# A retention layer followed by a mixture of attention experts: a new order of work in the head, at one step in the middle, and in the tail

## The chip, the cores and the metric

The kernel runs on one core of one Trainium2 chip. Its engines work side by side, each through its own instructions in program order: PE (matmuls), DVE, ACT and POOL (elementwise work), SP (which here only issues DMA transfers). What is measured is the time of one execution on the device in microseconds (us); lower is better.

## The reference

Eight batches of 576 tokens, eight heads of 64. First a retention layer, that is linear attention with a decay and no softmax; its output, 512 wide, is the input of a layer of four attention experts, of which each token takes two, weighted by a gate.

```python
scale = 1.0 / np.sqrt(64)
scores = scale * (q @ k.transpose(0, 1, 3, 2))
Dmat = np.where(rel >= 0, gamma[:, None, None] ** rel, 0.0)    # rel = i - j
x = (scores * Dmat) @ v          # then heads side by side: [8, 576, 512]
logits = x @ w_gate              # 4 experts, the two largest, softmax over them
for e in range(4):
    q, k, v = x @ wq[e], x @ wk[e], x @ wv[e]
    s = np.where(causal, -1e9, (q @ k.transpose(0, 2, 1)) / 8)
    a = np.exp(s - s.max(-1)); a /= a.sum(-1)
    out += chosen_weight[e] * (a @ v @ wo[e])
```

## The kernel before, in words

**Order.** Every engine runs its instructions in the order in which the program writes them; waits between engines are semaphores set from the tiles that are read and written. PSUM is a pool of eight banks that all stages take in turn (`bank`), so a matmul can also wait for a bank whose last reader isn't done. What stands where is decided by hand: a head written out line by line, a loop over n = 4 to 36 with a table of what each step does (`TILES` for scores, `STEPS` for the rest), and a `tail` written out again. Generators (`yield`) cut a stage in pieces, and `run`, `next` and `beside` say where a piece goes.

**Retention.** The batches go in four pairs, the tokens of a pair in nine steps of 128 columns, 36 steps in all. For a step n, `load(n)` brings x (queries and keys) and vk (values and keys) by DMA into three buffers each. `qk` multiplies keys by queries, ACT copies the result p, POOL sets it to zero above the diagonal (`affine_select`, L130). `decay` scales vk by powers of gamma (L95: DVE up to step 5, POOL later), `state` multiplies it to a state st, which DVE adds to the running state s (L111, L113). `result` has PE multiply the old state by the queries (old) and p by the values (own), adds the two (ACT L158, DVE L173), multiplies by the table gi (L178: DVE for n up to 2, POOL later) and splits the result in xh (ACT L181) and its remainder xl (L183), since a matmul takes rounded inputs: every product with x or a weight is done as hi·hi + lo·hi + hi·lo. `build` fills gi step by step on ACT (L136).

**Experts.** Three groups R of 384 tokens to a pair. `fetch(w)` brings a weight into a part of the tile TA, `weights(w)` splits it (whk, wlk and so on: hi on ACT L209, lo on DVE L211). `proj` makes k and q (pj, L226), `vproj` v and the gate's logits (pv, L251), `gate` the weights of the experts on DVE in two parts, `gates(0)` and `gates(1)`. v goes out to memory (hv) and comes back turned (`back`: vq<-hv, four DMA issues on SP). A batch b has five tiles t of queries; `score` computes scores (ss, L354, for t = 4 L360), DVE masks them and finds the minimum (L369, nm), ACT takes exps with their sums (L377). A step later `factors` makes the factors on DVE, `scale` multiplies the rows by them on ACT (L395), `turn` transposes blocks of 32x32 on DVE into TA and TB (L403, L405). `values(b, s0, s1)` multiplies them by vq for all five tiles at once (ys, L418, 144 matmuls for the whole batch, of which each leaves two rows in the trace), ACT rounds the result to yh (L424), DVE takes the remainder yl (L425); of an even batch POOL copies the last half block to the front of the next (L428). `outproj(n)` multiplies 128 columns of y by the output weights (po, L440), ACT copies them to ot (L448) and SP sends them out.

**Cold PE.** `warm(6)` issues six dummy matmuls (pw, L69) on a bank of their own.

## Time and profile before

| | |
|---|---|
| median of three executions | 425.62 us (425.48 to 428.55) |
| profiled execution | 426.58 us |
| its span, first to last instruction | 424.7 us |
| mean granted clock of PE | 0.988 of full |
| PE busy | 393.2 us, 93% |
| ACT, DVE, POOL busy | 283.4, 265.3, 167.3 us |
| moved by DMA | 65.10 MB, 153 GB/s |

The profile is of one execution, which has its own time; it lies 0.96 us over the median. The span is counted from the first instruction to the last; 1.88 us lie around it. A share of busy time is a mean over stages: head, loop and tail have different limits.

### The profile page before, as it was taken

To read this page: it belongs to the slowest core of one execution; us is meant where nothing else is said; L and a number is where in the kernel's file an instruction comes from. 1 tells how busy PE (TensorE), PEld (TensorE's weight loads), DVE (VectorE), ACT (ScalarE), POOL (GpSimd) and SP (SyncE) were. 2 spreads that over 40 slices of the span, in tenths; PEclk is the share of its full clock that TensorE was granted. 3 is DMA by queue.
4 is the path that set the end of the run, shared out by engine and by line. 5 is a ranking of instruction groups with operands and counts; after the bars stand their busy time and mean duration, and the time that the engine had idled before them with its cause. 6 is when DMAs were issued, how large, how long until landed. Compare 5 with 4: busy or idle time off the path is not lost.

```text
span 424.7 us, 20358 instructions
## 1 busy us (share of the span) xinstructions
PE 393.2 (93%) x8742; PEld 333.8 (79%) x8742; DVE 265.3 (62%) x1103; ACT 283.4 (67%) x809; POOL 167.3 (39%) x182
## 2 busy tenths in 40 slices
PE   7597999996799999999998989999999999999894
PEld 3486898796688978897887978898788987887673
DVE  2745386765777726869296727677497726983931
ACT  4354469674597747878576747779587747797751
POOL 2217856443345534445354444444445432000000
PEclk9898999998999999999999999999999999999999
DMA  8568557464255536567264635566454221422331
GB/s 288 164 235 323 172 187 184 131 185 131 102 168 159 191 101 174 165 176 243 98 166 135 188 127 158 183 174 199 145 169 146 86 75 42 115 66 96 105 119 60
DMA packets 33689, 65.10 MB, mean 153 GB/s; under 512 B 3392, under 2 KB 19264, under 8 KB 33600
## 3 DMA queue, kind: packets, MB, share of 16 engines
q1 hardware_dynamic: 32304, 59.08, 44.4%
q10 hardware_dynamic: 1296, 4.72, 3.2%
q8 instruction: 69, 1.13, 1.2%
q14 instruction: 20, 0.16, 0.2%
HBM read 49.63 MB, written 14.16 MB: 150 GB/s over the span
## 4 chain that ended last, share of the span: by engine, by line
PE 83%; DVE 6%; issue 5%; DMA 3%; ACT 1%; SPq 1%; ACTq 1%; DVEq 0%
PE pj L226 25%; PE pv L251 13%; PE ys L418 12%; PE po L440 10%; PE ss L354 7%; PE qk L124 4%; PE own L168 4%; DMA vk<-vkf 3%; PE old L155 3%; PE st L106 3%; PE ss L360 2%; DVE yl L425 1%; DVE x L173 1%; DVE ta L403 1%; DVE p L369 1%
## 5 line engine op out<-in xcount | busy, mean ns | idle before, releaser
L377 ACT ACTIVATE p<-p,nm 128x64 f32<-128x64 f32 (+5 forms) x144 | 79.3, 552 | 18.0 <-DVE nm L369 13.4
L130 POOL TENSOR_SCALAR_AFFINE_SELECT p<-p 64x512 f32<-64x512 f32 x72 | 49.0, 680 | 95.4 <-ACT p L127 93.0
L395 ACT ACTIVATE p<-p,sm 128x64 f32<-128x64 f32 (+5 forms) x144 | 69.4, 567 | 9.5 <-DVE sm L389 5.6
L183 POOL TENSOR_TENSOR xl<-x,xh 128x512 fp32r<-128x512 f32 x33 | 42.4, 1284 | 60.5 <-ACT xh L181 60.5
L369 DVE CUSTOM_DVE_ANT_0 p<-ss,mask 128x128 f32<-128x128 f32 (+7 forms) x128 | 50.4, 452 | 4.4 <-PE ss L354 4.3
L173 DVE TENSOR_TENSOR x<-x,own 128x256 f32<-128x256 f32 (+1 forms) x72 | 25.5, 386 | 43.0 <-ACT x L158 35.7
L425 DVE TENSOR_TENSOR yl<-ys,yh 128x288 fp32r<-128x288 f32 (+2 forms) x36 | 12.8, 417 | 61.6 <-ACT yh L424 61.6
L178 POOL TENSOR_TENSOR x<-x,gi 128x512 f32<-128x512 f32 x33 | 42.5, 1289 | 18.2 <-DVE x L173 11.3
L403 DVE STREAM_TRANSPOSE ta<-p 128x256 f32<-128x256 f32 (+2 forms) x144 | 48.9, 367 | 0.2 <-ACT p L395 0.2
L418 PE MATMUL ys<-ta,vq 32*64 32x288 f32 (+6 forms) x1152 | 45.4, 365 | 3.8 <-issue 3.8
L418 PE MATMUL ys<-tb,vq 32*64 32x96 f32 (+4 forms) x1344 | 43.5, 248 | 5.0 <-issue 5.0
L418 PEld LDWEIGHTS ys<-tb,vq 32*64 32x64 f32 x1344 | 39.3, 134 | 7.2 <-issue 6.3
L418 PEld LDWEIGHTS ys<-ta,vq 32*64 32x64 f32 x1152 | 36.0, 133 | 8.4 <-issue 7.2
L354 PE MATMUL ss<-k,q 64*64 64x512 f32 (+7 forms) x512 | 38.5, 406 | 0.2 <-issue 0.2
L424 ACT ACTIVATE yh<-ys 128x288 fp32r<-128x288 f32 (+2 forms) x36 | 10.9, 389 | 38.1 <-PE ys L418 38.1
L448 ACT ACTIVATE ot<-po 128x512 f32<-128x512 f32 x35 | 19.9, 592 | 19.8 <-PE po L440 16.2
L95 POOL TENSOR_TENSOR vk<-vk,con 128x512 f32<-128x512 f32 x30 | 31.5, 1051 | 0.0
L127 ACT ACTIVATE p<-qk 128x256 f32<-128x256 f32 x72 | 23.7, 382 | 9.3 <-PE qk L124 8.3
L181 ACT ACTIVATE xh<-x 128x512 fp32r<-128x512 f32 x36 | 22.3, 618 | 10.5 <-POOL x L178 8.6
L106 PE MATMUL st<-vk 64*64 64x64 f32 x1024 | 24.1, 220 | 5.6 <-DVE vk L95 4.0
L113 DVE TENSOR_TENSOR s<-st,s 128x128 f32<-128x128 f32 x112 | 24.9, 281 | 6.2 <-PE st L106 6.2
L168 PE MATMUL own<-p,vk 64*64 64x64 f32 x1152 | 26.4, 222 | 2.0 <-issue 1.9
(86 smaller groups left out, 892.0 us busy)
## 6 DMA issues: line engine op xcount, KB each, us to landing
x<-xf SPq DMA_DIRECT2D x33, 512.0 KB, 4.5
vk<-vkf SPq DMA_DIRECT2D x33, 512.0 KB, 5.7
vq<-hv SPq DMA_DIRECT2D x48, 192.0 KB, 6.3
out<-ot SPq DMA_DIRECT2D x36, 256.0 KB, 2.3
hv<-vn SPq DMA_DIRECT2D x24, 192.0 KB, 2.6
ta<-wraw ACTq DMA_DIRECT2D x3, 512.0 KB, 5.6
x<-xf ACTq DMA_DIRECT2D x3, 512.0 KB, 4.3
vk<-vkf ACTq DMA_DIRECT2D x3, 512.0 KB, 6.2
```

What stands on the lines that cost most here:

```text
L130: gp.affine_select(w, w, pattern=[[0, 8], [1, 64]], base=0, channel_multiplier=-1, compare_op=OP.is_ge, fill=0.0)
L168: mm(own[r][HALF[u], g, i], vk[HALF[r], s, 0, 2 * g + u], p[HALF[r], g, s, u], start=True, stop=True)
L178: e.tensor_mul(x32, x32, gi[:, :, t0:t0 + 128])
L226: mm(ps, ww[:, kc, p * 128:(p + 1) * 128], xx[:, kc], start=(i == 0), stop=(i == 11))
L251: mm(ps, xx[:, kc, l0:l0 + 128], ww[:, kc], start=(i == 0), stop=(i == 11))
L354: mm(ps[u][HALF[p]], q(p, z, i), k[p][HALF[z], :ws[u]], start=True, stop=True)
L369: v.tensor_tensor_reduce(x, ps[u], mask[:, 512 - ws[u]:], -1.0, BIG, OP.add, OP.min, nm[:, u:u + 1])
L377: act(x, x, AF.Exp, bias=bias, scale=-1.0, accum_out=sm[:, 0, u:u + 1])
L395: act(x, x, AF.Copy, scale=sm[:, 1, u:u + 1])
L403: v.transpose(TA[:, :min(nb, 8), z, k], x[:, :min(nb, 8)])
L418: mm(py[g][HALF[z], sj - s0:], vq[QUAD[g], jj, D * z:D * z + D], tt[QUAD[g]], start=(m == 0), stop=(m == 2 * s1 - 1))
L440: mm(ps, yy[:, p], ww[:, p], start=(i == 0), stop=(i == 5))
```

## The change

**Head.** `state(1)` and `state(2)` are written ahead of the last parts of `result(0)` and `result(1)`, so their adds on DVE stand before the multiplication by gi and the remainder. On ACT, which also issues DMAs in the head, load(5) and the fetch of v's weights stand behind the first evacuation of k; before, that fetch stood ahead of it, and load(5) behind the four builds of gi. ACT from load(4) on, before (x_354 and k_420, q_422 are the step's x, k and q):

```order
L81 DMA x<-xf 128x1024
L85 DMA vk<-vkf 128x1024
L198 DMA ta<-wraw 128x1024
L235 ACTIVATE k_420<-pj 128x384
L238 ACTIVATE q_422<-pj 128x384
L127 ACTIVATE p<-qk 128x256 x2
L235 ACTIVATE k_421<-pj 128x384
L136 ACTIVATE gi<-gi,con 128x128 x4
L81 DMA x<-xf 128x1024
L85 DMA vk<-vkf 128x1024
```

And now:

```order
L83 DMA x<-xf 128x1024
L87 DMA vk<-vkf 128x1024
L241 ACTIVATE k_416<-pj 128x384
L83 DMA x<-xf 128x1024
L87 DMA vk<-vkf 128x1024
L200 DMA ta<-wraw 128x1024
L244 ACTIVATE q_418<-pj 128x384
L129 ACTIVATE p<-qk 128x256 x2
L241 ACTIVATE k_417<-pj 128x384
L138 ACTIVATE gi<-gi,con 128x128 x4
```

The second pair of x and vk issues has moved up five rows, the fetch (ta<-wraw) down three. On DVE the same head, from step 0's last sum on, before:

```order
L173 TENSOR_TENSOR x_175<-x_175,own 128x2x64
L178 TENSOR_TENSOR x_175<-x_175,gi 128x512
L113 TENSOR_TENSOR s<-st,s 128x128 x4
L95 TENSOR_TENSOR vk<-vk,con 128x2x256
L183 TENSOR_TENSOR xl<-x_175,xh 128x4x128
L173 TENSOR_TENSOR x_263<-x_263,own 128x2x128 x2
L178 TENSOR_TENSOR x_263<-x_263,gi 128x512
L183 TENSOR_TENSOR xl<-x_263,xh 128x4x128
L113 TENSOR_TENSOR s<-st,s 128x128 x4
```

And now:

```order
L175 TENSOR_TENSOR x_176<-x_176,own 128x2x64
L115 TENSOR_TENSOR s<-st,s 128x128 x4
L180 TENSOR_TENSOR x_176<-x_176,gi 128x512
L97 TENSOR_TENSOR vk<-vk,con 128x2x256
L185 TENSOR_TENSOR xl<-x_176,xh 128x4x128
L175 TENSOR_TENSOR x_264<-x_264,own 128x2x128 x2
L115 TENSOR_TENSOR s<-st,s 128x128 x4
L180 TENSOR_TENSOR x_264<-x_264,gi 128x512
L185 TENSOR_TENSOR xl<-x_264,xh 128x4x128
```

Both adds of s have moved ahead of gi and xl of the step before.

**Step 12.** It is the first step with a values stage (batch 0), and its old tile is (0, 4). The four transposes of that tile now stand right behind the scales, ahead of masking the new tile's scores and of the gates. At step 13 the table puts the output projection ahead of the projections. DVE at step 12, the end of what stood before the transposes (p_1658 is the old tile; sixteen rows of masks and minima, L369, are above these):

```order
L293 TENSOR_TENSOR gd<-vn 128x48
L295 SCALAR_TENSOR_TENSOR gc<-gd,con 128x12x4 x2
L298 TENSOR_REDUCE rk<-gc 128x12
L300 TENSOR_REDUCE mx<-vn 128x3
L302 TENSOR_TENSOR ex<-vn,mx 128x12
L403 STREAM_TRANSPOSE ta<-p_1658 128x8x32
L405 STREAM_TRANSPOSE tb<-p_1658 128x10x32
```

And now, from the adds of the state on (p_1655 is the old tile, p_1851 the new one):

```order
L115 TENSOR_TENSOR s<-st,s 128x128 x4
L422 STREAM_TRANSPOSE ta<-p_1655 128x8x32
L424 STREAM_TRANSPOSE tb<-p_1655 128x10x32
L422 STREAM_TRANSPOSE ta<-p_1655 128x8x32
L424 STREAM_TRANSPOSE tb<-p_1655 128x10x32
L384 ISA p_1851,nm<-ss,mask 128x64
```

The transposes come before the first mask (ISA rows) instead of behind the gates.

**Tail.** Batch 6's y gets tiles of its own (`YY`, in the buffers of x's halves), batch 7's transposes too (`TT`, in the place of the weights of k and q, which are now one tile wkq, and of gi, now 3200 wide); scores of tile (7,3) go into spare x buffers and those of (7,4) into spare vk buffers (`units`). So no stage of batch 7 has to wait for batch 6's tiles. Scores of (7,2) and (7,3) stand ahead of values(6); tile (7,2) is scaled on POOL (`scale(b, t, gp)`, four multiplications by a broadcast column); output projections are redistributed; values(7) is one stage of 144 matmuls with one output projection in its middle, instead of two (96 for the first six half tiles, 144 narrower ones for the last three); one of the two warm(6) goes. PE around the scores of (7,3), before:

```order
L418 MATMUL ys<-tb,vq 64x160 x16
L354 MATMUL ss<-k_6688,q_7232 64x448 x2
L354 MATMUL ss<-k_6689,q_7233 64x448 x2
L354 MATMUL ss<-k_6688,q_7232 64x512 x2
L354 MATMUL ss<-k_6689,q_7233 64x512 x2
L360 MATMUL ss<-k_6688,q_7232 64x288 x2
L360 MATMUL ss<-k_6689,q_7233 64x288 x2
```

And now:

```order
L257 MATMUL pv<-whv,xl 128x260 x4
L369 MATMUL ss<-k_6685,q_7229 64x448 x2
L369 MATMUL ss<-k_6686,q_7230 64x448 x2
L369 MATMUL ss<-k_6685,q_7229 64x512 x2
L369 MATMUL ss<-k_6686,q_7230 64x512 x2
L438 MATMUL ys<-ta,vq 64x288 x8
L438 MATMUL ys<-tb,vq 64x32 x8
```

The scores of (7,3) stood behind all of values(6) and with those of (7,4) in one row; now they stand ahead of it, and those of (7,4) stay behind.

The diff:

```diff
...
-    gi = const.tile([128, 4, S + 64], F32, name="gi")
+    gi_all = const.tile([128, 3200], F32, name="gi")
+    gi = gi_all[:, :4 * (S + 64)].rearrange("p (k t) -> p k t", k=4)
+    wkq = sa.tile([128, 4608], F32R, name="wkq", bufs=1)
     con = const.tile([128, 92], F32, name="con")
...
         if "h" in parts:
-            W[n] = [const.tile([128, kc, wt], F32R, name="w" + y + n) for y in "hl"]
+            if n in "kq":
+                W[n] = [wkq[:, 1024 * z:1024 * z + 1024].rearrange("p (k w) -> p k w", k=kc)
+                        for z in range(2 * "kq".index(n), 2 * "kq".index(n) + 2)]
+            else:
+                W[n] = [const.tile([128, kc, wt], F32R, name="w" + y + n) for y in "hl"]
         hi, lo = W[n]
...
-    def scores(*tiles, name="p32", bufs=2):
-        size = sum((E if t < 4 else 2) * (CH[t][0] + CH[t][1]) for b, t in tiles)
-        buf, at, soft = sb.tile([128, size], F32, name=name, tag=name, bufs=bufs), 0, []
+    TT, YY = {}, {}
+
+    def scores(*tiles, units=None):
+        if not units:
+            size = sum((E if t < 4 else 2) * (CH[t][0] + CH[t][1]) for b, t in tiles)
+            buf, at, units = sb.tile([128, size], F32, name="p32", tag="p32", bufs=2), 0, []
+            for b, t in tiles:
+                w = CH[t][0] + CH[t][1]
+                for u in range(E if t < 4 else 2):
+                    units.append(buf[:, at:at + w])
+                    at += w
+        soft = []
         for b, t in tiles:
-            n, w = E if t < 4 else 2, CH[t][0] + CH[t][1]
-            soft.append(score(b, t, buf[:, at:at + n * w].rearrange("p (n w) -> p n w", n=n)))
-            at += n * w
+            n = E if t < 4 else 2
+            soft.append(score(b, t, units[:n]))
+            units = units[n:]
         yield
...
                         mm(ps[j][z][HALF[p]], q(p, z, 0), k[p][HALF[z], 288 * j:288 * j + 288], start=True, stop=True)
-        sm = sb.tile([128, 2, E], F32, name="sm", tag="sm", bufs=4)
-        nm = sb.tile([128, E], F32, name="nm", tag="nm", bufs=4)
+        sm = sb.tile([128, 2, E], F32, name="sm", tag="sm", bufs=5)
+        nm = sb.tile([128, E], F32, name="nm", tag="nm", bufs=5)
         SS[b, t] = (p32, sm, ws)
...
             for u in range(n):
-                x = p32[:, u, :ws[u]]
+                x = p32[u][:, :ws[u]]
                 if t < 4:
...
-    def scale(b, t):
+    def scale(b, t, e=None):
         p32, sm, ws = SS[b, t]
         for u, w in enumerate(ws):
-            x = p32[:, u, :w]
-            act(x, x, AF.Copy, scale=sm[:, 1, u:u + 1])
+            x = p32[u][:, :w]
+            if e:
+                e.tensor_mul(x, x, sm[:, 1, u:u + 1].to_broadcast([128, w]))
+            else:
+                act(x, x, AF.Copy, scale=sm[:, 1, u:u + 1])
             yield
...
             z, k, nb = u % 2, 2 * t + u // 2, w // 32
-            x = p32[:, u, :w].rearrange("p (j c) -> p j c", c=32)
-            v.transpose(TA[:, :min(nb, 8), z, k], x[:, :min(nb, 8)])
+            x = p32[u][:, :w].rearrange("p (j c) -> p j c", c=32)
+            ta, tb = TT.get(b, (TA, TB))
+            v.transpose(ta[:, :min(nb, 8), z, k], x[:, :min(nb, 8)])
             if nb > 8:
-                v.transpose(TB[:, :nb - 8, z, k - 4], x[:, 8:])
+                v.transpose(tb[:, :nb - 8, z, k - 4], x[:, 8:])
             yield
-    def values(b, s0, s1, cut=True):
+    def values(b, s0, s1, part=99):
         py = [bank([128, s1 - s0, 32], "ys") for g in range(4)]
...
             for z in range(2):
-                tt = TA[:, j, z, sj:s1] if j < 8 else TB[:, j - 8, z, sj - 4:s1 - 4]
+                ta, tb = TT.get(b, (TA, TB))
+                tt = ta[:, j, z, sj:s1] if j < 8 else tb[:, j - 8, z, sj - 4:s1 - 4]
                 for g in range(4):
...
                        start=(m == 0), stop=(m == 2 * s1 - 1))
-            if cut and m % 6 == 5 and m < 2 * s1 - 1:
+            if m % part == part - 1 and m < 2 * s1 - 1:
                 yield
         for g in range(4):
-            hi, lo = (y[:, g // 2, 1 + s0:1 + s1, g % 2] for y in YS)
+            hi, lo = (y[:, g // 2, 1 + s0:1 + s1, g % 2] for y in YY.get(b, YS))
             act(hi, py[g], AF.Copy)
...
         if b % 2 == 0:
-            for y in YS:
-                gp.tensor_copy(y[:, :, 0], f(y[:, :, 9]))
+            for y, z in zip(YY.get(b, YS), YS):
+                gp.tensor_copy(z[:, :, 0], f(y[:, :, 9]))
         yield
...
         l0 = 64 + 128 * c if c < 4 else 128 * (c - 4)
-        yh, yl = (y.rearrange("p a s b c -> p a (s b c)")[:, :, l0:l0 + 128] for y in YS)
+        ys = YY.get(2 * (n // 9) + (c >= 4), YS)
+        yh, yl = (y.rearrange("p a s b c -> p a (s b c)")[:, :, l0:l0 + 128] for y in ys)
         woh, wol = W["o"]
...
     for n in STEPS:
-        STEPS[n].sort(key=lambda x: "kvyob".index(x[0][0]))
+        STEPS[n].sort(key=lambda x: ("okvyb" if n == 13 else "kvyob").index(x[0][0]))
...
         todo = STEPS.get(n, [])
-        vals = [values(x[1], 0, 9, False) for x in todo if x[0] == "y"]
+        vals = [values(x[1], 0, 9) for x in todo if x[0] == "y"]
         bring = [x[1] for x in todo if x[0] == "back"]
...
         beside(vproj(R, 1), soft)
+        t2 = scores((b + 1, 2))
+        next(t2)
         beside(vproj(R, 2), soft)
...
         run(turn(b, 4))
-        run(outs(n - 4))
+        def flat(t):
+            return t.rearrange("p a b c -> p (a b c)")
+
+        xs = [flat(ld.tile([128, 2, 4, 128], F32, name="x", tag="x", bufs=3)) for z in range(2)]
+        vs = [ld.tile([128, 2, 2, 4, D], F32, name="vk", tag="vk", bufs=3).rearrange("p a b c d -> p (a b c d)")
+              for z in range(2)]
+        ys2 = [sa.tile([128, 4, NB], F32R, name="x" + y, bufs=2).rearrange("p a b -> p (a b)") for y in "hl"]
+        YY[b] = [y[:, :1280].rearrange("p (a s b c) -> p a s b c", a=2, s=10, b=2) for y in ys2]
+        ta2 = sa.tile([128, 4608], F32, name="wkq", bufs=1)
+        TT[b + 1] = (ta2.rearrange("p (j z s c) -> p j z s c", j=8, z=2, s=9),
+                     gi_all.rearrange("p (j z s c) -> p j z s c", j=10, z=2, s=5))
+
+        t3 = scores((b + 1, 3), units=[xs[u // 2][:, 512 * (u % 2):512 * (u % 2) + 512] for u in range(4)])
+        next(t3)
+        ys = values(b, 0, 9, 9)
+        next(ys)
+        held = outproj(n - 4, False)
+        next(held)
+        run(t2)
         gates(0)
-        soft = scores((b + 1, 2))
-        next(soft)
-        run(soft)
+        run(t3)
+        run(held)
         gates(1)
-        for t in range(3):
+        for t in range(4):
             factors(b + 1, t)
-        ys = values(b, 0, 9)
-        next(ys)
         run(scale(b + 1, 0))
-        run(outs(n - 3))
-        next(ys)
         run(scale(b + 1, 1))
-        run(scale(b + 1, 2))
-        run(outs(n - 2, n - 1))
-        next(ys)
-        back(R)
+        run(scale(b + 1, 2, gp))
         run(turn(b + 1, 0))
         run(turn(b + 1, 1))
-        soft, last = scores((b + 1, 3)), scores((b + 1, 4), name="p4", bufs=1)
-        next(soft)
-        next(last)
-        run(soft)
-        run(outs(n, n + 1))
+        next(ys)
+        run(ys)
+        back(R)
+        run(outs(n - 3))
+        t4 = scores((b + 1, 4), units=[x[:, :576] for x in vs])
+        next(t4)
+        run(t4)
+        run(scale(b + 1, 3))
         run(turn(b + 1, 2))
-        factors(b + 1, 3)
-        run(scale(b + 1, 3))
-        run(last)
-        ys = values(b + 1, 0, 6)
-        held = [outproj(c, False) for c in (n + 2, n + 3)]
-        for x in held:
-            next(x)
-        turns = turn(b + 1, 3)
-        for i in range(3):
-            next(turns)
-        run(ys)
-        for x in held:
-            run(x)
-        warm(6)
+        run(outs(n - 2))
         factors(b + 1, 4)
         run(scale(b + 1, 4))
-        run(turns)
-        last = turn(b + 1, 4)
-        run(outs(n + 4))
-        run(last)
-        ys = values(b + 1, 6, 9)
-        run(outs(n + 5))
+        run(turn(b + 1, 3))
+        run(outs(n - 1))
+        run(turn(b + 1, 4))
+        run(outs(n, n + 1, n + 2))
+        ys = values(b + 1, 0, 9, 9)
         next(ys)
-        run(outs(n + 6))
+        run(outs(n + 3))
         run(ys)
         warm(6)
-        run(outs(n + 7, n + 8))
+        run(outs(n + 4, n + 5, n + 6, n + 7, n + 8))
...
     fetch("q", nc.scalar)
+    state(1)
     next(late)
-    state(1)
     decay(2)
...
     qk(2)
+    state(2)
     next(late)
     run(late)
-    state(2)
...
     load(4, nc.scalar)
-    fetch("v", nc.scalar)
     weights("k", "l")
...
     run(proj(0, "k", 0))
+    load(5, nc.scalar)
+    fetch("v", nc.scalar)
     run(proj(0, "q", 0))
...
     build(3)
-    load(5, nc.scalar)
     decay(4)
...
             run(each(scale, old))
+            turns = each(turn, old)
+            if n == 12:
+                run(turns)
             run(soft)
...
             weights(w)
-        turns = each(turn, old)
-        if n == 12:
-            run(turns)
         hold = any(w[0] == "y" for w in STEPS.get(n, []))
         for _ in work(n):
-            if not hold:
+            if n >= LAG and not hold:
                 next(turns, None)
-        run(turns)
+        if n >= LAG:
+            run(turns)
         if n < NC:
...
     tail()
```

## Rows read from the trace of the kernel before

**Rows 1.** The page: busy time of the five engines (share of the span, instructions), and the share of each engine in the chain of work that ended last.

```profile
PE 393.2 (93%) x8742; PEld 333.8 (79%) x8742; DVE 265.3 (62%) x1103; ACT 283.4 (67%) x809; POOL 167.3 (39%) x182
...
PE 83%; DVE 6%; issue 5%; DMA 3%; ACT 1%; SPq 1%; ACTq 1%; DVEq 0%
```

**Rows 2.** One line of the waits of PE: which group of matmuls, what ended the wait, us in all, how often, the longest.

```profile
PE ys L418 <- issue: 8.8, 6, 3.8
```

**Rows 3.** The chain in order of time, around step 12 and then around a values stage of a later pair: start, us, what.

```profile
96.83 3.71 issue
100.54 7.84 PE ys L418 x186
...
348.57 0.43 issue
```

**Rows 4.** Windows of the same two places: stretch, length, then busy us (instructions) of PE, of its weight loads, of DVE, ACT and POOL where they did anything, the granted clock of PE, the DMA share and GB/s.

```profile
100.00:102.00 2.00, 1.46 (x26) 1.49 (x33) 1.55 (x5) 1.28 (x6) 0.65 (x1) 0.73 0.19 78
102.00:104.00 2.00, 2.00 (x65) 2.00 (x58) 0.00 (x0) 0.00 (x0) 0.62 (x1) 0.50 0.00 0
...
342.90:349.50 6.60, 6.17 (x290) 5.51 (x289) 0.00 (x0) 1.47 (x6) 1.27 (x1) 1.00 0.23 61
```

**Rows 5.** The timeline of DVE and ACT at step 12: start, us, engine, line, operation, tiles, shapes, count.

```profile
96.21 0.88 DVE L113 TENSOR_TENSOR s<-st,s 128x128 f32<-128x128 f32 x4
100.00 0.44 DVE L403 STREAM_TRANSPOSE ta<-p 128x256 f32<-128x256 f32 x1
...
95.31 1.46 ACT L395 ACTIVATE p<-p,sm 128x576 f32<-128x576 f32 x2
```

**Rows 6.** The chain in order of time in the head (ACTq is ACT's DMA issuing).

```profile
13.21 1.07 issue
...
15.90 0.70 DVE x L178
...
18.37 0.21 DVE s L113
...
22.91 4.53 PE pj L226 x24
...
30.79 7.25 DMA vk<-vkf
...
40.26 0.63 DVE wlv L211
40.93 3.54 PE pv L251 x20
...
49.73 0.87 issue
```

**Rows 7.** A window in the head, columns as in Rows 4.

```profile
40.00:42.00 2.00, 1.78 (x9) 1.48 (x8) 2.00 (x9) 0.00 (x0) 1.94 (x3) 0.50 0.88 332
```

**Rows 8.** The timeline of PE and of POOL in the head; in brackets the idle time before a row and what ended it.

```profile
38.85 0.69 PE L106 MATMUL st<-vk 64*64 64x64 f32 x32 [2.12 <-DVE vk L95]
...
50.84 0.69 PE L106 MATMUL st<-vk 64*64 64x64 f32 x32
...
16.36 1.47 POOL L130 TENSOR_SCALAR_AFFINE_SELECT p<-p 64x512 f32<-64x512 f32 x2 [3.46 <-ACT p L127]
...
48.60 1.04 POOL L95 TENSOR_TENSOR vk<-vk,con 128x512 f32<-128x512 f32 x1
```

**Rows 9.** The chain in order of time in the tail.

```profile
380.22 2.22 PE ys L418 x64
...
384.02 2.06 PE ys L418 x72
...
389.06 1.91 PE ys L418 x94
...
395.70 5.83 PE po L440 x24
401.53 3.51 PE ys L418 x118
405.04 1.40 PE pw L69 x6
...
409.24 1.32 PE ys L418 x62
...
412.14 2.05 PE ys L418 x122
414.19 1.76 issue
415.95 0.80 PE ys L418 x38
```

**Rows 10.** The timeline of PE at a gap of the tail, and of ACT; in brackets the idle time before a row and what ended it.

```profile
395.70 0.71 PE L440 MATMUL po<-who,yh 128*128 128x512 f32 x2 [2.00 <-DVE nm L369]
...
385.15 3.51 ACT L395 ACTIVATE p<-p,sm 128x192 f32<-128x192 f32 x8
```

**Rows 11.** Groups of instructions by form on POOL (busy us, mean ns of one, idle before) and one group of DVE (shortest, median and longest ns, first and last start, forms).

```profile
L95 POOL TENSOR_TENSOR vk<-vk,con 128x512 f32<-128x512 f32 x30 | 31.5, 1051 | 0.0
L178 POOL TENSOR_TENSOR x<-x,gi 128x512 f32<-128x512 f32 x33 | 42.5, 1289 | 18.2 <-DVE x L173 11.3 <-ACT p L395 3.9
...
L403 DVE STREAM_TRANSPOSE ta<-p x144: 200/402/446, 63.2 to 408.7; 128x256 f32<-128x256 f32 x96, 128x64 f32<-128x64 f32 x16, 128x128 f32<-128x128 f32 x16, 128x192 f32<-128x192 f32 x16
```

## The prediction

> **What bounds the kernel now.** First the page's table of engines and the shares of its chain [rows 1]: the matmul engine PE is busy 393.2 of 424.7 us, and 83% of the chain that ended last is its own work. A gain is therefore a gap in PE that goes, PE work that goes, or PE work that runs at the full clock instead of half. Next PE's waits [rows 2]: 8.8 us ahead of the matmuls of ys, of which one gap of 3.8 takes nearly half. Then the chain and the windows around the three places that the diff touches: step 12 [rows 3 to 5], the head [rows 6 to 8], the tail [rows 9 to 11].
>
> **Step 12: a gap and its cold restart.** PE ends its scores at 96.83 and starts ys at 100.54; the 3.71 between are put down to "issue" [rows 3]. The rows of DVE and ACT say what it is [rows 5]: the last scale of the old tile ended on ACT at 95.31 + 1.46 = 96.77, and the first transpose that ys reads runs on DVE only at 100.00 to 100.44, because 16 rows of masking and five of gates stand before it. ys starts 0.10 after that. PE comes back from the gap at half its clock (1.2 of 2.4 GHz): 0.73 and 0.50 in the two windows of 2 us after it, against 1.00 in the stretch of another batch's ys [rows 4]. So the ys here take 7.84 us [rows 3], and there 6.5 of a stretch of 6.60 [rows 4], a pause of 0.43 [rows 3] included.
> The change puts the four transposes right behind the state adds, which end at 96.21 + 0.88 = 97.09 [rows 5]. The first ends at about 97.5, the fourth, at 0.4 each, at 98.7; ys goes through one half of the transposes after the other and so need not wait again. PE's gap shrinks from 3.71 to about 0.7, after which I expect no cold stretch, as there is none after the pause of 0.43 at 348.57 [rows 3, 4]: ys from 97.5 to 104.1 instead of 108.38, that is 4.2. The masks and gates on DVE move 1.7 later; the exps that follow end later than before, but the next reader of them is a step away. The same work follows (ys evacuated, its remainder, the projections), so it moves as a whole; I keep back 0.3 for the masks and take **-3.9** (-2.6 if the restart is as cold as before, 97.5 + 7.84 = 105.34 against 108.38, and the masks cost 0.4; -4.4 if both are free).
>
> **Head.** Two edits. (a) The adds of state 1 and 2 go ahead of the multiplication by gi and of xl on DVE. old(2) waits for the add at 18.37, which stands behind x·gi (15.90) and xl [rows 6]. Ahead of them it ends near 16.3, some 2.2 sooner. But own(2) then waits for the triangle mask on POOL, which ran 16.36 to 17.83 [rows 8], so that about 1.2 arrive at the first proj (22.91 [rows 6]). By my schedule PE now waits in two places of some 2 ahead of it; if it starts proj at half its clock, as it did the ys from 100.54 to some 104 [rows 3, 4], 3.6 us at half speed lose up to 1.8.
> (b) load(5) is issued on ACT's queue before the fetch of v's weights, two evacuations earlier. In the chain its transfer runs from 30.79 for 7.25, to 38.04, and DVE's decay follows at once [rows 6]; st waits 2.12 for that [rows 8], and the clock falls to 0.50 at 40 to 42 [rows 7]. Issued near 25, it has landed by about 32, and st(5) has nothing to wait for. What is late next: the weights of v (their fetch is now behind it); wlv ended on DVE at 40.26 + 0.63 and pv started at 40.93 [rows 6]. I put wlv, no longer behind the late decay, near 37.9, so pv starts some 3 sooner and, without the gap, warm. Then POOL bounds: its decays, masks and results are nearly back to back until 54, the decay of 1.04 at 48.60 ends 1.2 before its st at 50.84 [rows 8], and it can be no more than about 2.1 sooner. That limits the gain at 51 to some 3.3, whatever (a) gives. I take **-3.0**; with (a) and POOL both against it -1.0, with neither -4.3.
> The order at step 13 (output projection ahead of proj), the buffers 4 to 5 and one tile for the four weights change no PE work; the matmuls that they move stand in full rows either way: 0.
>
> **Tail.** From the chain [rows 9], all on PE:
> - values(7) in one piece: before 3.51 + 1.32 + 2.05 + 0.80 = 7.68 for 96 + 144 = 240 matmuls; in one piece 144 as values(6), 2.22 + 2.06 + 1.91 = 6.19: -1.49.
> - one of two warm-ups of 6 dummies goes: -1.40.
> - po waits 2.00 for the mask of tile (7,3) [rows 10]. The scores of (7,2) and (7,3) now stand ahead of ys(6), and have PE work of 6.19 + 2 x 1.46 = 9.1 us after them: -2.00.
> - the gap of 1.76 put down to "issue" [rows 9] has every input long there. Such pauses of PE without a wait stand all over the chain: 1.07 at 13.21 and 0.87 at 49.73 [rows 6], 0.43 at 348.57 [rows 3]. I expect not none but one of mean size, (1.07 + 0.87 + 0.43 + 1.76) / 4 = 1.03: -0.73.
> - new: ys(7) waits for the last transposes. From the scores of (7,4) on (about 390.8 by my schedule) DVE has 20 transposes at 0.40 or less [rows 11], about 7.4 with the factors between; PE has five output projections of 5.83 / 4 = 1.46 [rows 9], 7.3, of which it starts the first at once: +0.65. yh in one piece is wider: +0.10.
> Together **-4.9**. What is on other engines: of the eight scales that took ACT 3.51 us [rows 10], tiles (7,1) and (7,2), the four of (7,2) become broadcast multiplications on POOL; ACT, by my schedule, is busy with exps and scales from 380 to 389, when values(6) ends. POOL shows no multiplication by a broadcast column; the nearest rows are its decay, also by a broadcast operand, 1.05 us for 512 wide, and x·gi, 1.29 [rows 11]. For 2 x 320 and 2 x 384, that is 2.9 to 3.5; their inputs are there at about 385.9 and DVE is due at 392.9, so 3.5 of 7.0 are left: no cost. SP's queue: out(n-4) and four vq loads stand ahead of twelve outs, all issued before PE's last row; their 2.3 us end within the same 3.8 after PE as before. Ends of the tail: -3.2 (two pauses, 1.3 of wait) to -6.5 (no pause, no wait).
> The Trainium skill (Runtime: NRT & Kernel Launch, section Instruction fetch mechanics) says that an engine's instructions are streamed in blocks of 256 and that crossing a block is "mostly hidden". The pauses here, if they are such crossings, are not hidden, up to 1.76 us; by the rule the sum would be 1.0 better, at -12.8.
>
> **Sum:** -3.9 - 3.0 - 4.9 = -11.8. The profiled execution, 426.58 (span 424.7 and 1.88 around it), becomes 414.8; the median of the three, 425.62, becomes **413.8**, which I forecast.
>
> **Rivals.**
> 1. The head gives little. For it: its PE waits on four engines in turn, and a removed wait shows the next (POOL's mask, wlv). Against it: both edits start the very thing that was late. Then the head gives -0.8 and the kernel takes 416.0.
> 2. The tail gives half. DVE has to do all the transposes of batch 7 in one run, and ACT must do exps and scales of three tiles in the time that PE takes for five projections; ys(7) in one piece can start only after the last of them, where before it started with the early ones. 1.3 of wait instead of 0.65, two pauses instead of one, and 0.5 of late evacuations: -2.7, and 416.0. Blocking by POOL's rows would come on top: a transpose held up for each of four multiplications of about 0.8 loses 2 to 3 us on DVE, some 2 on PE. Against it: L403's 144 rows go from 200 to 446 ns [rows 11], none held up for the length of a POOL row, though POOL works beside many of them.
> The Trainium skill (SBUF — State Buffer, section Who interferes with whom) tells of a pair of ports that GpSimd and some DVE operations take by an exclusive lock, so that the later one "fully blocks". The rows of the transposes don't show it; by it the time would be about 415.8.
> 3. Step 12's gap is what it is called, a stop of instruction supply, and not the transposes: then it stays (0), and 417.7. Against it: ys starts 0.10 after the transpose.
> 4. Slower: the broadcast multiplications on POOL take several times their nearest row. DVE's transposes of (7,2) stand ahead of those of (7,3) and (7,4) in its order, so ys(7) waits for POOL's fourth. Slack 3.5; from 385.9 + 4t > 392.9 + 11.8, that is t > 4.7 us each, it eats all gains; from 3.65 the kernel is within 1% of before, from 5.8 slower by over 1%: 430. For it: no such row in the trace. Against it: five times the decay's 1.05.
>
> **Chances.** Forecast 0.45; rival 1 0.14; rival 2 0.17; rival 3 0.07; two or three of these together 0.10, at 418.2 (1 and 2), 419.9 (3 with one of them) and 422.1 (all), half of it above 421.4 since each may also go further than its price; rival 4 0.07, of which 0.03 within 1% and 0.04 beyond. A measurement of this kernel tells about 1% from no change, 4.3 us. Faster than 421.4: 0.45 + 0.14 + 0.17 + 0.07 + 0.05 = 0.88; within 1% 0.05 + 0.03 = 0.08; slower 0.04. The three lower ends add up to -4.4 - 4.3 - 6.5 = -15.2, 410.4; the spread of the runs before takes some tenths more: 410. On the other side rivals 1 to 3 and their pairs lie within 420. Left out are 0.12 above and some 0.05 around the two ends.
>
> **What would show it.** In the profile after: no idle of 3 us ahead of ys near 97, its matmuls done in 6.2 to 6.6 at clock 1.00; st(5) without an idle before it and wlv the last that pv waits for; POOL's multiplications at 0.7 to 0.95; ys(7) in one stretch of 6.2 with a wait under 1 for DVE. It would be wrong if ys(7) waits over 2 for transposes, if PE's clock falls below 1 in proj at 21 to 26, or if pauses of over 1 us stand in three places of the tail.

## The result, and the profile after

The changed kernel takes 415.6 us (median of five, 411.74 to 421.38) where the kernel before, run beside it, takes 428.55: a ratio of 0.9695, 95% interval 0.9613 to 0.9777. Forecast were 413.8 against 425.62, a ratio of 0.972. A second comparison on another chip gave 0.9707 (0.9659 to 0.9755; 414.25 against 427.29). Executions of over 1.5% above a kernel's fastest are left out of the ratios, and a difference in us given from here on is a ratio applied to the median of the kernel before. The execution profiled in the first comparison happened to be the longest of its five, so the rows here are of the one profiled in the second: 413.74, its span 412.0 where before it was 424.7. Line numbers have moved by 2 to 21: transposes are L422, ys L438, po L461, masks L384, st L108, pv L257, pj L232.

The page of the changed kernel, its engines and its row of PE's granted clock in 40 slices of the span, in tenths:

```profile
PE 387.3 (94%) x8544; PEld 327.3 (79%) x8544; DVE 266.7 (65%) x1099; ACT 280.5 (68%) x801; POOL 169.1 (41%) x186
...
PEclk9999999999999999999999999999999999999999
```

The line of PE's waits that answers to [rows 2] (us in all, times, longest):

```profile
PE ys L438 <- issue: 4.7, 6, 1.1
```

PE's busy time is 5.9 us less [rows 1], and no slice of its clock is below 9.

The chain in order of time, head, step 12 and tail (start, us, what); these rows answer to [rows 3], [rows 6] and [rows 9]:

```profile
12.42 2.19 issue
...
21.49 4.46 PE pj L232 x24
...
37.01 0.51 DVE wlv L217
...
37.88 2.68 PE pv L257 x20
...
42.61 2.04 issue
...
93.83 0.67 issue
94.50 5.13 PE ys L438 x127
99.62 0.83 issue
100.46 1.63 PE ys L438 x79
102.09 0.40 ACT yh L444
...
373.76 3.37 PE ys L438 x90
...
378.73 2.67 PE ys L438 x132
...
391.25 0.12 issue
391.37 3.89 PE ys L438 x86
...
396.85 2.93 PE ys L438 x127
```

Windows of step 12 and of the head, columns as in [rows 4]; these answer to [rows 4] and [rows 7]:

```profile
100.00:102.00 2.00, 1.54 (x79) 1.33 (x78) 0.00 (x0) 0.00 (x0) 1.03 (x1) 1.00 0.03 8
...
40.00:42.00 2.00, 2.00 (x101) 1.86 (x99) 0.00 (x0) 0.95 (x3) 1.26 (x2) 1.00 0.72 283
```

The timeline at step 12 (DVE), at the state matmuls of the head (PE) and at the scales of tile (7,2) (POOL); these answer to [rows 5], [rows 8] and [rows 11]:

```profile
93.17 0.88 DVE L115 TENSOR_TENSOR s<-st,s 128x128 f32<-128x128 f32 x4
93.96 0.43 DVE L422 STREAM_TRANSPOSE ta<-p 128x256 f32<-128x256 f32 x1
...
48.85 0.69 PE L108 MATMUL st<-vk 64*64 64x64 f32 x32
...
379.46 2.97 POOL L411 TENSOR_TENSOR p<-p,sm 128x320 f32<-128x320 f32 x4 [27.62 <-ACT ot L469]
```

**Where the 12.7 us of the span went**, from the chains of both traces (before, then after):

| stretch | before | after | difference |
|---|---|---|---|
| start to the state matmuls of [rows 8] | 50.84 | 48.85 | -1.99 |
| from there to the end of step 12's scores | 45.99 | 44.98 | -1.01 |
| to the end of its ys | 11.55 | 8.26 | -3.29 |
| to the tail's first pv | 263.34 | 262.60 | -0.74 |
| to the last evacuation of po | 49.29 | 43.58 | -5.71 |

The three places gave 2.0, 3.3 and 5.7 where 3.0, 3.9 and 4.9 were forecast. Another 1.75 lies in the two stretches between them, for which nothing was forecast; 0.6 of it is one stop, 1.50 at 73.75 before and 0.88 at 71.40 after. So it is in part luck that the sum, -11.8, came so near: two terms were too large, one too small, and 1.75 stands in none. The stops put down to "issue" are still there, at 12.42, 42.61 and 99.62 for instance, and they are where the terms missed.

### The profile page after: what moved, and what is told of

Its sections match the earlier page's. It is cut to its first block, busy times and chain, and to the rows that moved or that the text cites. A ratio compares the mean times of both kernels' runs of the same rounds, so it can differ in the third digit from the quotient of the medians.

```text
span 419.7 us, 19965 instructions
## 1 busy us (share of the span) xinstructions
PE 390.7 (93%) x8544; PEld 329.1 (78%) x8544; DVE 265.7 (63%) x1099; ACT 280.7 (67%) x801; POOL 169.2 (40%) x186
## 4 chain that ended last, share of the span: by engine, by line
PE 85%; DVE 5%; issue 5%; ACT 2%; DMA 2%; SPq 1%; POOL 0%; ACTq 0%; DVEq 0%
PE pj L232 25%; PE pv L257 13%; PE ys L438 12%; PE po L461 11%; PE ss L369 7%; PE qk L126 4%; PE own L170 4%; PE st L108 3%; PE old L157 3%; PE ss L375 2%; DMA vk<-vkf 2%; DVE x L175 1%; DVE s L115 0%; ACT xh L183 0%; DVE p L384 0%
## 5 line engine op out<-in xcount | busy, mean ns | idle before, releaser
L232 PE MATMUL pj<-xh,wkq 128*128 128x384 f32 x384 | 79.0, 347 | 2.0 <-ACT xh L183 1.0
L232 PEld LDWEIGHTS pj<-xh,wkq 128*128 128x128 f32 x384 | 66.7, 190 | 15.9 <-PE ss L369 5.7
L384 DVE CUSTOM_DVE_ANT_0 p<-ss,mask 128x64 f32<-128x64 f32 (+7 forms) x124 | 48.2, 444 | 5.2 <-PE ss L369 5.0
L445 DVE TENSOR_TENSOR yl<-ys,yh 128x288 fp32r<-128x288 f32 x28 | 10.9, 450 | 51.9 <-ACT yh L444 51.9
L422 DVE STREAM_TRANSPOSE ta<-p 128x256 f32<-128x256 f32 (+3 forms) x126 | 42.8, 367 | 0.0
L232 PE MATMUL pj<-xl,wkq 128*128 128x384 f32 x192 | 41.1, 334 | 0.0
L438 PE MATMUL ys<-tb,vq 32*64 32x32 f32 (+4 forms) x1120 | 35.8, 249 | 5.5 <-issue 5.5
L369 PE MATMUL ss<-k,q 64*64 64x512 f32 (+7 forms) x512 | 40.2, 420 | 0.7 <-issue 0.7
L438 PEld LDWEIGHTS ys<-tb,vq 32*64 32x64 f32 x1120 | 32.5, 131 | 8.6 <-issue 7.8
L438 PE MATMUL ys<-ta,vq 32*64 32x224 f32 (+3 forms) x896 | 37.5, 377 | 0.7 <-PE ss L369 0.4
L232 PEld LDWEIGHTS pj<-xl,wkq 128*128 128x128 f32 x192 | 34.0, 188 | 0.0
L108 PE MATMUL st<-vk 64*64 64x64 f32 x1024 | 25.0, 222 | 7.9 <-issue 5.6
L438 PEld LDWEIGHTS ys<-ta,vq 32*64 32x64 f32 x896 | 28.4, 130 | 3.7 <-issue 1.6
```

Of the source, the lines that this page charges most:

```text
L232: mm(ps, ww[:, kc, p * 128:(p + 1) * 128], xx[:, kc], start=(i == 0), stop=(i == 11))
L369: mm(ps[u][HALF[p]], q(p, z, i), k[p][HALF[z], :ws[u]], start=True, stop=True)
L384: v.tensor_tensor_reduce(x, ps[u], mask[:, 512 - ws[u]:], -1.0, BIG, OP.add, OP.min, nm[:, u:u + 1])
L422: v.transpose(ta[:, :min(nb, 8), z, k], x[:, :min(nb, 8)])
L438: mm(py[g][HALF[z], sj - s0:], vq[QUAD[g], jj, D * z:D * z + D], tt[QUAD[g]], start=(m == 0), stop=(m == 2 * s1 - 1))
```

## Experiments: the three parts alone

All of these are the kernel before with one part of the diff; the first two edits are

```diff
+    state(1)
     next(late)
-    state(1)
     decay(2)
...
+    state(2)
     next(late)
     run(late)
-    state(2)
...
-    fetch("v", nc.scalar)
...
     run(proj(0, "k", 0))
+    load(5, nc.scalar)
+    fetch("v", nc.scalar)
...
-    load(5, nc.scalar)
```

**The head alone.** 

> The kernel before with the head's two edits alone. Terms of the prediction: first pv behind wlv near 37.4 instead of 40.93, the state matmuls that stood at 50.84 near 48.8 or sooner, time -3.0 us (ratio 0.993). Rival, the stops of PE (put down to issue) eat it: the places are 2 or more sooner once stops are taken off, but the stops between 40 and 100 add up to 2 us more than the 2.4 of before, and the time is within 1 us of before.

Measured: 0.9939 (0.9908 to 0.9971), that is -2.6 us. The first proj starts at 21.58 instead of 22.91, pv at 37.40, near the 37.4 expected, st at 48.06 instead of 50.84. PE's stops between 40 and the scores of step 12 come to 1.6, where the rival wanted 2 more than the 2.4 of before: it falls.

**Step 12 alone.**

```diff
             run(each(scale, old))
+            turns = each(turn, old)
+            if n == 12:
+                run(turns)
             run(soft)
...
-        turns = each(turn, old)
-        if n == 12:
-            run(turns)
```

> The kernel before with the four transposes of step 12 moved ahead of the masks, and nothing else. Terms of the prediction: gap ahead of ys under 1 us, ys in 6.5 us at the full clock, the place behind ys 3.9 sooner against the scores ahead of it. Rival (instruction supply): gap under 1, clock 1.00, but ys holds two stops of about 1.1 each and takes 9 us from first to last, so the place is only about 2.0 sooner.

Measured: 0.9894 (0.983 to 0.9958), -4.5 us. Chain of this kernel at step 12:

```profile
95.77 0.76 issue
96.53 4.98 PE ys L418 x124
101.52 0.45 issue
...
103.60 0.40 ACT yh L424
```

From the end of the scores to the end of ys 7.83 instead of 11.55 [rows 3], -3.7: the gap is 0.76, and of the two stops of the rival there is one, of 0.45. This is one execution. In the six traces that have the new order at step 12, ys in one piece and no added transfers, the same stretch takes 7.9 to 10.0, mean 8.8, and the stops in ys come to between 0.45 and 2.75; the first trace of the changed kernel has the rival's two, 1.09 and 1.10, and ys takes 9.23. In the five traces with the old order it takes 10.3 to 11.7, mean 11.3, and four of the five ran ys at half clock at first. That is -2.5 on average (-2.7 without the first trace of the changed kernel, its longest execution): the rival's mechanism is there, beside that of the prediction.

**The tail alone** (the diff's hunks from `gi_all` to the end of `tail`, without step 13's order). 

> The kernel before with the tail's edits alone (and its tiles). Terms of the prediction: from the pv at 371.72 to the last matmul 49.2 us before, 44.3 here (-4.9), and the same in the time (ratio 0.988). Rival (no stop falls in the tail, as in the trace of the changed kernel): -6.0. Rival of new waits: -2.7, with a wait of over 1 us of ys behind the last transposes.

Measured: 0.9832 (0.9777 to 0.9886), -7.2 us. From the tail's first pv to the last matmul 43.38, with no stop and a wait of 0.12 ahead of ys(7), as in the changed kernel. The rest of the time is on the other side. In the five traces with the old tail this stretch takes 48.8, 49.4, 50.0, 50.6 and 52.4; in the seven with the new one and nothing else done to it 43.4 to 43.7. The trace of step 12 alone, which has the old tail, shows why the old one varies. Its chain after the gap of 1.99 ahead of po, and at the second gap:

```profile
390.36 7.36 PE po L440 x24
...
410.07 2.01 issue
```

Windows behind the two gaps; the granted clock is the third number from the end:

```profile
392.00:394.00 2.00, 2.00 (x7) 1.52 (x6) 2.00 (x9) 1.62 (x5) 0.00 (x0) 0.50 0.00 0
...
412.00:414.00 2.00, 1.92 (x43) 1.15 (x44) 0.41 (x3) 0.68 (x4) 0.00 (x0) 0.57 0.03 8
```

After either gap PE ran at half clock here; the same four po take 7.36 instead of the 5.83 of [rows 9], where the same gap had no such sequel. The five old tails go by this: 48.8 and 49.4 where neither gap had a stretch at half clock behind it, 50.0 and 50.6 where one had, 52.4 here, where both had. So the two gaps were worth more than their own 3.76 in some executions, and the trace that the forecast was read from was one of the mild ones. The means are 50.2 and 43.5, a difference of -6.8, most of the way from the -5.7 of that trace to the -7.2 of the time.

**All parts again.** 

> The changed kernel once more, beside the three parts on one chip. If the parts add up: its gain is the sum of the three gains, 9 to 12 us. If the stops of PE move from place to place as the order ahead of them changes, the sum of the parts misses it by 2 us or more either way, and its profiled execution has its stops elsewhere than in the first trace (there 3.88 us at 71.30).

Measured: 0.9707, -12.5 us, where the three parts sum to -14.3; their intervals are 1.3 to 2.7 wide to either side, so they add up as far as can be told. Both lie above the 9 to 12 that were expected, and the 1.8 between them, short of the 2 that was to tell of moving stops, is within the noise: the test decides nothing. The stop that took 3.88 at 71.30 in the first trace takes 0.88 at 71.40 in this one: same place in the program, other length.

## Experiments: inside the head and the tail

**The state adds alone.** 

> The kernel before with the state adds of the head moved ahead of gi and xl alone. Terms of the prediction: first proj 1.2 sooner, and little of it left at 50 us, because load(5) is still late (st waits for the decay as before): time -0.8 to 0. Rival: the whole of the head's gain (-2.6 to -3.0) comes from this edit.

Measured: 0.996 (0.9926 to 0.9993), -1.7 us, more than the -0.8 to 0 expected, though the interval reaches into it. The first proj starts 0.8 sooner, at 22.14, pv behind wlv at 40.04, and st still waits 2.01 for the late decay, as expected. At 51 nothing is left of it in this trace (51.29), for a stop of 2.96 stands just ahead. One thing differs from the kernel before: behind the same wait of 2 us the granted clock stays at 1.00 from 38 to 44, and pv isn't cold.

**load(5) alone.** 

> The kernel before with load(5) and the fetch of v exchanged alone. Terms of the prediction: st(5) no longer waits 2.1 for the decay, pv no longer runs cold: the place at 51 us is 2.2 sooner with stops taken off, time -2.2. Rival: the wait moves to wlv (v's weights fetched later), pv starts no sooner, time 0.

Measured: 0.9941 (0.9909 to 0.9974), -2.5 us. The chain of this kernel:

```profile
22.71 6.12 PE pj L226 x24
...
35.59 1.30 POOL x L178
...
39.90 0.63 DVE wlv L211
40.57 2.68 PE pv L251 x20
...
51.01 0.60 PE st L106 x32
```

The chain no longer holds the transfer of vk: it goes through x, xh and whv to wlv, and pv starts only 0.36 sooner than in [rows 6]. So the rival's mechanism is there, but this trace can't say how much of it is due to the missing (a): its first proj started cold, 6.12 for the rows that took 4.53 in [rows 6], and that alone makes x, wlv and pv later by 1.6. pv takes 2.68 instead of 3.54, with no gap of 2.12 ahead of it and the clock at 1.00; the kernel with the state adds alone had such a gap and no cold pv, so this is a cost that the gap has in some executions only. At st nothing is left (51.01), and where the 2.5 of the time come from this trace doesn't show. With both edits wlv ends at 37.5 and pv starts behind it at 37.88. Alone they sum to -4.2, together they give -2.6; with intervals of about 1.4 to either side that is no difference that could be told.

**Tile (7,2) scaled on ACT again.**

```diff
-        run(scale(b + 1, 2, gp))
+        run(scale(b + 1, 2))
```

> The changed kernel with tile (7,2) scaled on ACT again instead of POOL. By the prediction POOL's place costs nothing and takes about 1.8 us of ACT away in a stretch where ACT is busy until values(6) ends: the tail is 0 to 1.5 longer. Rival (POOL holds up DVE's transposes beside it, the lock): the tail is shorter by up to 2, and the transposes of (7,0) and (7,1) are faster here than in the changed kernel.

Measured: 0.9762 (0.9716 to 0.9807) against 0.9707 on another chip, where the intervals overlap, so the time alone doesn't tell. In the one trace the tail is 45.31 instead of 43.65 or 43.38: 1.7 to 1.9 longer, a little over the range. PE waits twice:

```profile
388.28 0.71 PE L375 MATMUL ss<-k,q 64*64 64x288 f32 x6 [0.62 <-DVE xl L445]
...
396.81 1.10 PE L438 MATMUL ys<-wkq,vq 32*64 32x288 f32 x12 [0.69 <-DVE wkq L422]
```

Eight transposes in the timeline of DVE, in the changed kernel beside POOL's multiplications:

```profile
380.12 2.32 DVE L422 STREAM_TRANSPOSE wkq<-p 128x64 f32<-128x64 f32 x8
```

And here, with POOL idle:

```profile
383.29 2.71 DVE L422 STREAM_TRANSPOSE wkq<-p 128x64 f32<-128x64 f32 x8
```

They are not held up by POOL; the rival of the lock falls for this operation.

**Step 13 in the old order.**

```diff
-        STEPS[n].sort(key=lambda x: ("okvyb" if n == 13 else "kvyob").index(x[0][0]))
+        STEPS[n].sort(key=lambda x: "kvyob".index(x[0][0]))
```

> The changed kernel with step 13 in the old order (projections ahead of the output projection). By the prediction 0. Rival: the wait of 1.5 us of PE ahead of step 13's first long matmuls is for a bank that DVE frees late; a projection waits for the same bank, so it stays and the time is the same; if it goes, the time is 1 to 1.5 less.

Measured: 0.9734 (0.9678 to 0.979), not to be told from 0.9707. The wait for DVE's x stays ahead of the projection, 0.66 in this trace instead of 1.52 ahead of po.

## Experiments: what stops PE

The stops are put down to "issue": PE waits for nothing the profile shows. The trace also has the transfers of instruction queues; the page of the changed kernel counts them (packets, MB, share of the DMA engines):

```profile
q8 instruction: 67, 1.10, 1.2%
```

These are 67 blocks of 16,384 bytes. With 8544 matmuls, as many weight loads and 237 others, PE has 17,325 rows in the trace, which makes 67 blocks of 256 and a rest, so they are its instructions. In the second trace of the changed kernel PE has twelve stops of over 0.3 us that are put down to issue, and each ends 1.31 to 1.51 us after such a block has arrived; the stop at 99.62, for one, ends at 100.46, 1.31 after.

Counting PE's rows settles more. In the fourteen traces of this document 155 gaps of over 0.3 us ahead of matmuls are put down to issue. Ahead of the end of 150 of them stands a whole number of 256 rows and 193 or 194 more: always the same place in a block, its border. The other five are the gap ahead of ys at step 12 in the five kernels with the old order there, each 28 rows past a whole number. So that gap is no stop of instruction supply, already by the trace of the kernel before, and the others are.

**More traffic.** Changed kernel, with

```diff
             load(n + 2)
+            if n == 12:
+                for z in range(4):
+                    junk = hbm.tile([128, 2, 4, 128], F32, name=f"junk{z}", bufs=1)
+                    nc.sync.dma_start(junk, xf[z])
```

> The changed kernel with four extra copies of 512 KB in memory, issued on SP behind load(14) at step 12, so that transfers are in flight while ys runs; nothing reads them. If PE's stops are late blocks of instructions, which go over the same DMA engines: the stops in and behind ys at step 12 (0.8 to 1.1 each before) grow to 2 or more, and each still ends about 1.4 us after a block has arrived. If they are something else (banks, a wait that the profile does not show): they stay at 0.8 to 1.1.

Measured: 0.987 (0.9807 to 0.9933). Its chain at step 12:

```profile
95.92 4.98 PE ys L438 x124
100.90 3.63 issue
```

Two windows there; the last three numbers are granted clock, DMA share and GB/s:

```profile
102.00:104.00 2.00, 0.00 (x0) 0.00 (x0) 0.00 (x0) 0.00 (x0) 0.46 (x1) 0.75 0.81 336
104.00:106.00 2.00, 1.47 (x48) 1.42 (x55) 0.00 (x0) 0.00 (x0) 0.00 (x0) 0.50 0.07 25
```

The stop has grown from 0.83 to 3.63, at the same place in the program, while transfers take 0.81 of the DMA engines; it ends 1.38 after its block has arrived, and PE comes back at half clock. The block's own transfer is no longer (0.98 against 1.04), but it starts 1.26 after PE has stopped, where in the changed kernel it started 1.51 before. The stop is the block that is late. Of the two stops expected to grow only this one did; the one behind ys, 0.92 before, is gone: PE, slowed to half clock, needs that block only 1.9 after it has arrived (106.61).

**ys(7) not cut.**

```diff
-        ys = values(b + 1, 0, 9, 9)
-        next(ys)
-        run(outs(n + 3))
+        ys = values(b + 1, 0, 9)
         run(ys)
+        run(outs(n + 3))
```

> The changed kernel with values(7) not cut: its 144 matmuls in a row, the output projection from their middle behind them. Instruction supply: one stop of 0.8 to 1.8 comes back in ys(7), the tail is 43.4 + 1 to 1.8. If the cut does nothing: the tail is the same, or shorter, since the evacuation of ys starts a projection sooner.

Its chain at ys(7):

```profile
393.81 4.98 PE ys L438 x130
398.80 1.81 issue
400.61 1.57 PE ys L438 x62
```

A stop of 1.81, and the tail is 45.11 instead of 43.65: the cut is what keeps the stop away. The time, 0.9861 (0.9805 to 0.9916), is further from 0.9707 than 1.5 us; but in the profiled execution the span's difference of 3.9 is all there: 1.5 in the tail and 2.4 ahead of it, in the head, where the two kernels are the same. There the first proj starts later (23.02 against 21.49) and cold, 6.06 against 4.46.

**The same for the values stages of the loop.** Step 12 first, then all of them, in six pieces (in `spread_all` the cut is 3 for every n, and the last test in `vals[...]` reads `n != 12` alone):

```diff
-            add(4, ("kq", R, 0))
+            add(3 if P_ == 1 else 4, ("kq", R, 0))
-        vals = [values(x[1], 0, 9) for x in todo if x[0] == "y"]
+        vals = [values(x[1], 0, 9, 3 if n == 12 else 99) for x in todo if x[0] == "y"]
+        if n == 12:
+            next(vals[0])
...
+                        if n == 12:
+                            next(vals[0], None)
                         i += 1
-                        for y in vals[:i == 3]:
+                        for y in vals[:i == 3 and n != 12]:
...
             if n == 12:
                 run(turns)
+                next(late)
```

> The changed kernel with step 12's ys cut in six pieces and the first projections of step 13 set between them (xh of the step before earlier on ACT); the work is the same. Instruction supply: the stops in ys go (-1 to -2 us at this place), since a block of 256 instructions then lasts longer than its fetch; time -1 to -2 against the changed kernel. If the stops have another cause, they stay and the time is the same, or 1 more since the projections wait for xh.

> The same for all values stages of the loop, each in six pieces between the six pieces of a projection. Instruction supply: the stops in ys near 150, 203, 246, 299 and 341 (0.3 to 1.1 each in the changed kernel, 3.8 in all) go or shrink to under 1 in all; time -3 to -5 against the changed kernel. Rival: the evacuation of ys now ends a projection piece later and what follows waits; gain under 1.

Measured: 0.9755 (0.9709 to 0.9801) and 0.9984 (0.9945 to 1.0023): no gain, and with all of them the whole gain of the change is gone. The stops are gone as instruction supply has it, in all six stages. The chain of one stage in the changed kernel:

```profile
142.56 2.28 PE pj L232 x12
144.84 5.08 PE ys L438 x139
149.92 0.93 issue
150.85 1.03 PE ys L438 x47
```

The start of the same stage in pieces:

```profile
143.99 0.91 PE pj L232 x4
144.90 1.45 PE ys L438 x42
146.36 0.90 PE pj L232 x4
```

From the first projection to the end of the stage 11.61 in the one, 0.93 of it the stop, and 11.97 in the other with none. Without stops the changed kernel's five later stages take 10.67 to 10.85, those in pieces 11.95 to 12.15: about 1.2 more for nine more changes between the shapes of matmul (32x64 for ys, 128x128 for projections), 0.13 each if all of it is theirs. Part of it shows in the rows: four matmuls of a projection take 0.90, where twelve in a row take 2.28, that is 0.76 for four. The stops that this saves were 0.31 to 1.11. The Trainium skill (TensorEngine Tiling (Array Packing), section Key Properties) says that a change of tiling mode drains the engine; it gives no price, and these rows agree in kind. Of the 8.2 by which the two spans differ, 2.5 lie in those five stages and 2.2 from step 12 to the first of them, where st waits 2.05 for an evacuation; 4.4 lie between and behind the stages, and what makes them up is not shown (ahead of step 12 the kernel in pieces is 0.8 shorter).

## Why the prediction was right, point by point

- **Step 12, forecast -3.9: right in its cause, too large in size by the traces.** The gap fell from 3.71 to 0.67 and the clock stayed at 1.00, so the transposes were what ys waited for, and rival 3 falls; the count of rows says the same. The term that was mis-sized is ys in 6.5: at full clock it takes 7.1 to 9.8 in the six traces, for stops of 0.45 to 2.75 fall in it. At half clock its blocks had come in time. The measures are -3.3 (trace of the whole), -3.7 (trace of the part), -2.5 (means of all traces) and -4.5 with 2.7 to either side (time of the part).
- **Head, forecast -3.0: right in size by the time, -2.6 (1.2 to 3.9) alone, and rival 1 (-0.8) lies outside that.** For (a) 1.2 was forecast at the first proj. It starts at 20.9 to 23.0 in the ten traces that have (a), mean 21.8, and at 21.8 to 23.6 in the four without, mean 22.7: -1.0, in ranges that overlap. In the changed kernel proj did not start cold (4.46 for its rows); in one of the ten it did. (b) was right on what is late next, wlv, which ended at 37.5 where 37.9 was written. Whether (b) alone brings pv forward by as much stays open. The place at 51 us moved by 1.99, where at most 3.3 and in the sum 3.0 stood, and over all traces by 1.8 (mean 49.0 in nine with both edits, 50.8 in three with neither); in the trace of the whole more stops took the rest (2.19 and 2.04 in the chain, 1.07 and 0.87 before).
- **Tail, forecast -4.9: too small, -5.7 by the trace and -7.2 (4.9 to 9.5) by the time.** The step that failed is "I expect not none but one of mean size": the output projection in the middle of ys(7) keeps the stop away (0 instead of 1.03), which the test with an uncut ys shows. The wait for the last transposes was 0.12 instead of 0.65, and values(7) took 3.89 + 2.93 = 6.82 instead of 6.19 (uncut 4.98 + 1.57 = 6.55 without its stop). These three make -1.0, -0.5 and +0.6, which brings -4.9 to -5.8. POOL's four rows took 2.97 (forecast 2.9 to 3.5), and its place is worth 1.7 us of tail by the one trace without it: rival 4 falls. So does rival 2: of its three prices none was paid.
- **The base.** The sum was made against one execution, whose two gaps in the tail had no cold sequel. Other executions of that tail took up to 3 us longer and one 0.6 less, the new tail never more than 0.3. That lies outside the sum, and it is the most likely reason why the tail measures more by the time than by that trace.
- **The pauses.** The row of mean size was a guess at a cause that the page doesn't name. The Trainium skill's "mostly hidden" (Runtime: NRT & Kernel Launch, Instruction fetch mechanics) doesn't hold here: a stop takes up to 2.19 us in the rows above, 3.88 in the first trace, and 3.63 beside extra transfers.

## What to carry to other kernels

When PE stops with nothing to wait for, look at the instruction queue's transfers: if a block arrives about 1.4 us before the stop ends, and the stop stands a whole number of blocks behind another one, the stretch issues instructions faster than they come, and one long matmul stage in the middle of it (as in values(7)) costs less than the stop; six such cuts cost more. A gap that is closed is worth its length and, in some executions, a cold restart besides, so a forecast from a single trace should look at whether the gaps it removes had one there. Before pricing two edits one by one, follow what is late next with only one of them in place.

## What the runs showed of the hardware

- Instruction blocks of PE: 256 instructions each, and a stop ends 1.31 to 1.51 us after one has arrived (twelve stops). In ys, 576 instructions in 6.2 us use one up in 2.8 us; from the end of the stop at 100.46 to the end of the next, at 103.85, are 3.4 and 256 rows.
- A gap of PE is followed by half clock in some executions and not in others: four of the five gaps of 3.2 to 3.8 ahead of ys at step 12 were, and three of the five of 2.0 ahead of po in the old tail.
- Changing the shape of the matmuls costs about 0.13 us each time, an estimate from the stages in pieces (11.95 to 12.15 against 10.67 to 10.85).
- DVE's multiplication of vk by a broadcast operand takes 0.68 in the head by itself, and 1.78 where it starts 0.06 after a multiplication of 1.29 on POOL. The timelines of DVE and POOL in the kernel with load(5) alone:

```profile
33.23 0.68 DVE L95 TENSOR_TENSOR vk<-vk,con 128x512 f32<-128x512 f32 x1
...
35.65 1.78 DVE L95 TENSOR_TENSOR vk<-vk,con 128x512 f32<-128x512 f32 x1
...
35.59 1.29 POOL L178 TENSOR_TENSOR x<-x,gi 128x512 f32<-128x512 f32 x1
```

  The POOL row ends at 36.88, the DVE row 0.55 later, as if it had stood still till then. In all ten traces with load(5) early this row takes 1.76 to 1.78. The trace of the kernel before has such a row too, DVE's remainder, which starts 0.18 after a mask on POOL and takes 1.02 instead of 0.69:

```profile
17.35 1.02 DVE L183 TENSOR_TENSOR xl<-x,xh 128x512 fp32r<-128x512 f32 x1 [0.76 <-ACT xh L181]
```

  Where DVE starts first, its row takes 0.69 (vk at 38.06 in the kernel before, a mask on POOL 0.42 later). That is the lock of the Trainium skill (SBUF — State Buffer, Who interferes with whom), for an operation with two inputs in SBUF; the transposes, with one, did not show it. The prediction had tested the rule on transposes alone, and priced it for them at 415.8; the same section leaves out a DVE operation with at most one input in SBUF, unless it runs in a two-port mode, so that price is not what it says of them.
